# Clustered attention and a gated FFN on one core: from a hand-written step calendar to an operation graph that a list scheduler orders

## The chip, the cores and the metric

The kernel runs on one core of one Trainium2 chip. The metric is the device time of one launch in microseconds (us). The kernel before takes 378.75 us, the median of three runs (378.61 to 380.31). One execution was also recorded by the hardware profiler; all rows below are from that one, with a span of 378.3 us.

## What is computed

Four batches (B) of eight heads (H), 768 tokens (S), head size 64 (D). A query may attend to a key only when both pick the same one of 16 cluster centroids. The attention output, heads side by side, goes through a feed-forward network (FFN) with a sigmoid gate: 512 to 1536 and back to 512.

```
q_assign = argmax(q_n . c_n);  k_assign = argmax(k_n . c_n)      # normalised vectors
mask     = q_assign[:, :, :, None] == k_assign[:, :, None, :]
scores   = where(mask, q @ k.T / 8, -1e9)
attn     = softmax(scores) @ v
x        = attn, heads beside each other: (3072, 512)
out      = (sigmoid(x @ w_gate) * (x @ w_val)) @ w_out           # float32
```

## The kernel before

Tokens lie 128 to a partition block, so a head has six blocks of keys and six of queries. Two heads make a pair, four pairs a batch.

**Preparing a pair.** The raw keys and queries are split into a fp16 high part and a fp16 low part that lie beside each other in a tile `hl`: DVE makes the high part, POOL subtracts to get the low one (L212 and L215 in batch 0, L631 and L632 later). A DMA transpose from the SP queue turns `hl` to `T` (L222): 64 rows of high part, 64 of low part, tokens along the free axis. PE multiplies `T` with the centroids (`logits`, L229 and L238). DVE takes the maximum over 16 clusters and marks it as a one-hot `oh` (L256 to L265); the mark of a query is inverted and scaled by -1920. `oh` is turned too: by PE and a copy in batch 0 (L283, L530, L552), by a DMA transpose in the other batches (L645). Four small DMAs, `hop` (L287), then put 16 rows of it into rows 64 to 79 of `T`, over a part of the low rows that is no longer needed. A matmul over 80 rows then gives the scores with the mask in them.

**A step** is one block of 128 keys against three blocks of queries: one scores matmul of 384 columns (L419), one exponential of 128x384 on ACT (L424), and three matmuls with the values (L436) two steps later. There are 96 steps in a batch and 384 in all. At the end of a head DVE adds a tiny sum of all values (`sv`), takes the reciprocal (L197, L199), and POOL multiplies (L202). After a pair, SP issues a DMA transpose of the result into `xT` (L444).

**Batch 0** is cut in two. Steps 0 to 47 (A) use the first half of the queries, steps 48 to 95 (B) the second half. Each half has its own splits, DMA transposes (eight of nine blocks for A, four of six blocks for B), logits and hops. The very first pair puts its marks in place by PE and two copies instead of hops (`first_place`, L513 to L517).

**FFN.** It works on 384 tokens at a time, eight such halves in all. A gate unit (L301) is four matmuls of 384 columns, followed by a tanh on ACT (L307); a value unit (L316) likewise, followed by a multiplication on DVE (L321); there are 12 of each in a half. Then come nine output units of four matmuls of 512 columns (L333), and after every third one a copy (ACT L342 or DVE L340) and a store from SP (L343). Units are kept in a queue, and `ffn_run` issues some after every step, in proportion to the backlog.

**What sets the order.** Every engine runs its instructions in the order in which the program writes them. That order is written by hand: `run_steps` walks over the steps, and `at(i, f)` enters background work for step number i. Loads, DMA transposes, hops and stores all go through SP's one queue, weights and the first value loads through POOL's.

**PSUM** has eight banks: `ring` has four, `avp` two, `op` (FFN outputs) two.

Of the kernel before, what the change touches and what calls it, by code (L numbers as in the profile page):

```python
# [16 lines left out]
def kernel(  # L17
# [26 lines left out]

    def pool(name, bufs, **kw):
        return ctx.enter_context(
            tc.tile_pool(name=name, bufs=bufs, reuse_waits="tile", **kw)
        )
# [3 lines left out]
    rawp = pool("raw", 4)  # L52
    hlp = pool("hl", 4)
    tp = pool("T", 10)
    tbp = pool("TB", 4)
    vap = pool("va", 6)
    svp = pool("sv", 6)
    ohp = pool("oh", 2)
    esp = pool("es", 6)
    tmpp = pool("tmp", 2)  # L60
    xpp = pool("xp", 3)
    xtp = pool("xT", 2)
    htp = pool("hT", 2)
    thp = pool("th", 3)
    osp = pool("os", 3)
    smp = pool("sm", 3)
    ring = pool("ring", 4, space=bass.MemoryType.PSUM)
    avp = pool("avp", 2, space=bass.MemoryType.PSUM)
    op = pool("op", 2, space=bass.MemoryType.PSUM)

    def bank(n=512, dt=FP, name="bank"):
        return ring.tile([128, n], dt, tag="ring", name=name)


    ident = const.tile([128, 128], FP, name="ident")
    make_identity(nc, ident)
    identh = const.tile([128, 128], HP, name="identh")
    warm = const.tile([128, 512], HP, name="warm")
    POOL.memset(warm, 0.0)
    ones = const.tile([128, 128], HP, name="ones")  # L80
    POOL.memset(ones, 1.0)

    def raw(side):
        return rawp.tile([128, 2, NCH, 64], FP, tag=f"{side}raw", name=f"{side}raw")

    SRC = {"q": q, "k": k, "v": v}

    def view(side, b, p):
        return SRC[side][b, 2 * p : 2 * p + 2].rearrange("h (p c) d -> p h c d", c=NCH)

    RAW = {}

    def load(eng, side, b, p):
        t = RAW[side, b, p] = raw(side)
        eng.dma_start(out=t, in_=view(side, b, p))

    cen = const.tile([128, D], FP, name="cen")
    load(SP, "k", 0, 0)
    load(ACT, "q", 0, 0)
    SP.dma_start(out=cen, in_=centroids.rearrange("h c d -> (h c) d"))  # L100
    load(SP, "k", 0, 1)
    load(ACT, "q", 0, 1)


    WQ = 3
# [6 lines left out]
    def load_w(i):  # L112
        for t, src in ((wg[i], moe_w_gate), (wv[i], moe_w_val)):
            POOL.dma_start(
                out=t.rearrange("p dc fc f -> p dc (fc f)"),
                in_=src.rearrange("(dc p) (g f) -> p dc g f", p=128, f=WQ * 128)[:, :, i, :],
            )

    def load_wo(i):
        POOL.dma_start(  # L120
            out=wo[i],
            in_=moe_w_out.rearrange("(g fc p) m -> p g fc m", g=2, p=128)[:, i],
        )

# [5 lines left out]
    r1 = const.tile([128, 1], FP, name="r1")  # L130
    cm = const.tile([128, H, 2, NCL], HP, name="cm")

    def centroid_a():
        DVE.tensor_tensor(sq, cen, cen, ALU.mult)
        DVE.tensor_reduce(ss, sq, AX.X, ALU.add)
        ACT.activation(r0, ss, AF.Sqrt)
        ACT.activation(r1, warm[:, 0:1], AF.Exp)

    def centroid_b():
        DVE.tensor_scalar(r0, r0, 1e-6, None, ALU.add)  # L140
        DVE.reciprocal(r0, r0)
        for i in range(2):
            DVE.tensor_scalar(c2[:, i, :], cen, r0, None, ALU.mult)
        ct_ps = bank(128, name="ct_ps")
        PE.transpose(ct_ps, c2.rearrange("p a d -> p (a d)"), ident)
        cv = ct_ps.rearrange("p (h c) -> p h c", c=NCL)
        ACT.copy(cm[:, :, 0, :], cv)
        DVE.tensor_tensor(cm[:, :, 1, :], cv, cm[:, :, 0, :], ALU.subtract)


    VA, SV = {}, {}

    def v_cast(b, p):
        va = vap.tile([128, 2, NCH, 65], HP, name="va")
        VA[b, p] = va
        POOL.memset(va[:, :, :, 64:65], 1.0)
        POOL.tensor_copy(va[:, :, :, 0:64], RAW["v", b, p])

    def v_sum(b, p):
        s = svp.tile([128, 2, 65], HP, tag="vs", name="vs")  # L160
        POOL.memset(s[:, :, 64:65], float(NCH))
        with nc.allow_low_precision("sums of the fp16 values' sources"):
            DVE.tensor_reduce(  # L163
                s[:, :, 0:64], RAW["v", b, p].rearrange("p h c d -> p h d c"), AX.X, ALU.add
            )

        def rest():
            t = bank(130, name="vs_ps")
            PE.matmul(
                out=t, lhsT=ones, rhs=s.rearrange("p h d -> p (h d)"), start=True, stop=True  # L170
            )
            sv = svp.tile([128, 2, 65], FP, tag="sv", name="sv")
            SV[b, p] = sv
            DVE.tensor_scalar(sv.rearrange("p h d -> p (h d)"), t, TINY, None, ALU.mult)

        return rest

    def v_sum_pe(b, p):
        t = bank(130, name="vs_ps")
        for j in range(NCH):  # L180
            PE.matmul(
                out=t.rearrange("p (h d) -> p h d", h=2), lhsT=ones, rhs=VA[b, p][:, :, j, :],
                start=(j == 0), stop=(j == NCH - 1),
            )
        sv = svp.tile([128, 2, 65], FP, tag="sv", name="sv")
        SV[b, p] = sv
        DVE.tensor_scalar(sv.rearrange("p h d -> p (h d)"), t, TINY, None, ALU.mult)


    def bcast(ap, n):  # L190
        return ap.unsqueeze(len(ap.shape)).to_broadcast(list(ap.shape) + [n])

    def normalise(av, nq, b, p, e, x, eng=None):

        t = tmpp.tile([128, NCH, 65], FP, name="t")
        sv = SV[b, p][:, e, :].unsqueeze(1).to_broadcast([128, nq, 65])
        DVE.tensor_tensor(t[:, 0:nq, :], av, sv, ALU.add)  # L197
        rec = smp.tile([128, NCH], FP, name="rec")
        DVE.reciprocal(  # L199
            rec[:, 0:nq], t[:, 0:nq, 64:65].rearrange("p c x -> p (c x)")  # L200
        )
        (eng or POOL).tensor_tensor(x, t[:, 0:nq, 0:64], bcast(rec[:, 0:nq], 64), ALU.mult)  # L202
# [3 lines left out]
    T = {}  # L206

    def split(n, parts, lo_eng):

        hl = hlp.tile([128, n, 128], HP, tag="hl", name="hl")  # L210
        for o, r in parts:
            DVE.tensor_copy(hl[:, o : o + r.shape[1], 0:64], r)  # L212
        for o, r in parts:
            m = r.shape[1]
            lo_eng.tensor_tensor(  # L215
                hl[:, o : o + m, 64:128], r, hl[:, o : o + m, 0:64], ALU.subtract
            )
        return hl

    def turn(key, hl, pl):  # L220
        T[key] = pl.tile([128, hl.shape[1], 128], HP, tag="T", name="T")
        SP.dma_start_transpose(out=T[key], in_=hl.rearrange("p c x -> p (c x)"))  # L222

    def logits2(groups):

        lg = bank(512, name="lg2")
        for i, (t, c, h) in enumerate(groups):
            for s in range(2):
                PE.matmul(  # L229
                    out=lg[:, bass.ts(i, NCL)], lhsT=t[:, c, :], rhs=cm[:, h, s, :],  # L230
                    start=(i == 0 and s == 0), stop=(s == 1), skip_group_check=True,
                )
        return lg[:, 0 : len(groups) * NCL].rearrange("p (c n) -> p c n", n=NCL)

    def logits(t, h, n):
        lg = bank(512, name="lg")
        for c in range(n):
            PE.matmul(  # L238
                out=lg[:, bass.ts(c, 32)], lhsT=t[:, c, :],
                rhs=cm[:, h].rearrange("p s n -> p (s n)"), start=True, stop=True,  # L240
            )
        lv = lg[:, 0 : n * 32].rearrange("p (c s n) -> p c s n", s=2, n=NCL)
        lo = smp.tile([128, 12, NCL], FP, name="lglo")
        ACT.copy(lo[:, 0:n], lv[:, :, 1, :])  # L244
        return lv[:, :, 0, :], lo[:, 0:n]

    def pick(lg, parts):

        if isinstance(lg, tuple):
            ls = smp.tile([128, 12, NCL], FP, name="lgs")  # L250
            n = lg[0].shape[1]
            DVE.tensor_tensor(ls[:, 0:n], lg[0], lg[1], ALU.add)  # L252
            lg = ls[:, 0:n]
        n = lg.shape[1]
        mx = smp.tile([128, 18], FP, name="mx")
        DVE.tensor_reduce(mx[:, 0:n], lg, AX.X, ALU.max)  # L256
        for a, z, nh, key, o in parts:
            DVE.tensor_tensor(
                o,
                lg[:, a:z].rearrange("p (h c) n -> p h c n", h=nh),  # L260
                bcast(mx[:, a:z].rearrange("p (h c) -> p h c", h=nh), NCL),
                ALU.is_equal if key else ALU.is_lt,
            )
            if not key:
# [454 lines left out]
```

## Time and profile before

| | |
|---|---|
| median of the three runs | 378.75 us |
| span of the profiled execution | 378.3 us |
| busy: PE, ACT, DVE, POOL | 337.0, 230.4, 176.7, 113.6 us |
| mean granted clock of PE | 0.932 |
| first scores matmul (step 0) starts | 21.05 us |
| step 24, 48, 72 | 43.61, 63.21, 92.10 us |
| step 96 (second batch), 192, 288 | 111.61, 170.94, 247.69 us |
| last step ends, last matmul ends | 319.5, 374.5 us |

A step is said to start where its scores matmul starts in the trace. A busy PE is not PE at its peak: its clock can be at half rate ("granted clock" 0.50), and a matmul then takes twice as long. So a stage is read by three things together: how much of it PE was busy, at which clock, and what ended the idle time.

### The profile page before, as it was taken

Reading aid. Unit: us, or ns where it says so; the run is one execution under the profiler, and the core shown is the slowest. Engines: PE = TensorE matmul, PEld = TensorE weight load, DVE = VectorE, ACT = ScalarE, POOL = GpSimd, SP = SyncE. Lnnn points to the kernel's source line nnn. Section 1 sums busy time; section 2 is a strip of 40 time slices with the busy share of each in tenths; the row PEclk is TensorE's granted clock in tenths of the full one; section 3 lists DMA queues with packets and bytes.
Section 4 is the critical chain, followed back from the end, with each engine's and each line's share of the span. In section 5 each row is a group of like instructions: output and inputs, shape, how many; then the busy total and the mean of one; then the engine's idle time right before and its main releaser. Section 6 shows DMA issues by size and latency. Waiting matters only on the chain.

```text
span 378.3 us, 8520 instructions
## 1 busy us (share of the span) xinstructions
PE 337.0 (89%) x3177; PEld 205.5 (54%) x3177; DVE 176.7 (47%) x455; ACT 230.4 (61%) x527; POOL 113.6 (30%) x179
## 2 busy tenths in 40 slices
PE   3786955669999989889999999999999999999995
PEld 1354633436655556554666566656665566565552
DVE  3463532225563675662656365635563333242230
ACT  3044744437867878875787778758777787232231
POOL 3756566103342634523242423232401000000000
PEclk9975875559999999999999999999999999999999
DMA  5967999974766976966566539653523120300102
GB/s 186 253 187 150 226 179 197 239 137 144 110 175 143 215 187 126 224 165 174 146 148 177 114 88 231 178 139 81 87 52 73 51 36 2 105 1 30 55 2 83
DMA packets 96858, 50.07 MB, mean 132 GB/s; under 512 B 75376, under 2 KB 93424, under 8 KB 96816
## 3 DMA queue, kind: packets, MB, share of 16 engines
q1 hardware_dynamic: 90032, 42.44, 48.0%
q0 software_dynamic: 6240, 6.29, 9.6%
q10 hardware_dynamic: 544, 0.79, 0.6%
q8 instruction: 25, 0.41, 0.4%
q14 instruction: 17, 0.14, 0.1%
HBM read 28.34 MB, written 6.29 MB: 92 GB/s over the span
## 4 chain that ended last, share of the span: by engine, by line
PE 68%; DMA 14%; DVE 7%; issue 4%; POOL 3%; ACT 1%; SPq 1%; POOLq 0%; DVEq 0%
PE o L333 16%; PE v L316 15%; PE g L301 15%; DMA T<-hl 12%; PE sc L419 11%; PE av L436 6%; PE lg L238 2%; DMA T<-ohT 2%; PE wm L489 2%; DMA cen<-in_centroids_dram 1%; DVE hT L321 1%; POOL hl L215 1%; DVE vs L163 1%; DVE hl L212 1%; DVE t L197 1%
## 5 line engine op out<-in xcount | busy, mean ns | idle before, releaser
L424 ACT ACTIVATE es<-sc 128x384 f16<-128x384 f32 x384 | 174.2, 492 | 67.6 <-PE sc L419 54.5
L419 PE MATMUL sc<-T 80*128 80x384 f16 x384 | 124.3, 348 | 5.8 <-DMA T<-ohT 4.5
L436 PEld LDWEIGHTS <-es 128*128 128x128 f16 x1152 | 84.6, 102 | 51.0 <-ACT es L424 6.1
L436 PE MATMUL av<-va,es 128*128 128x65 f16 x1152 | 102.3, 200 | 1.4 <-ACT es L424 0.7
L321 DVE SCALAR_TENSOR_TENSOR hT<-th,v 128x384 f16<-128x384 f32 x96 | 53.0, 552 | 94.8 <-PE av L436 56.1
L202 POOL TENSOR_TENSOR xp<-t,rec 128x384 f16<-128x384 f32 (+1 forms) x40 | 28.3, 707 | 146.2 <-DVE rec L199 119.2
L333 PE MATMUL o<-wo,hT 128*128 128x512 f16 x288 | 70.3, 378 | 0.0
L307 ACT ACTIVATE th<-g 128x384 f32<-128x384 f32 x96 | 47.2, 492 | 28.5 <-DVE hT L321 16.2
L301 PE MATMUL g<-xTb,wg 128*128 128x384 f16 x288 | 58.6, 325 | 0.5 <-DVE hT L321 0.2
L316 PE MATMUL v<-xTb,wv 128*128 128x384 f16 x288 | 58.6, 325 | 0.3 <-DVE hT L321 0.3
L301 PEld LDWEIGHTS <-wg 128*128 128x128 f16 x384 | 37.7, 98 | 24.0 <-issue 3.8
L316 PEld LDWEIGHTS <-wv 128*128 128x128 f16 x384 | 37.5, 98 | 22.7 <-issue 2.5
L333 PEld LDWEIGHTS <-hT 128*128 128x128 f16 x288 | 27.8, 97 | 26.1
L419 PEld LDWEIGHTS <-T 80*128 80x128 f16 x384 | 38.3, 100 | 5.4 <-DMA T<-ohT 4.2
L632 POOL TENSOR_TENSOR hl<-kraw,hl 128x384 f16<-128x384 f32 x24 | 22.0, 917 | 31.4 <-issue 24.8
L197 DVE TENSOR_TENSOR t<-av,sv 128x390 f32<-128x390 f32 (+1 forms) x40 | 19.2, 479 | 22.9 <-PE av L436 22.9
L632 POOL TENSOR_TENSOR hl<-qraw,hl 128x384 f16<-128x384 f32 x24 | 21.9, 913 | 20.7 <-DVE hl L631 20.5
L342 ACT ACTIVATE ob<-o 128x512 f32<-128x512 f32 x16 | 9.6, 597 | 22.6 <-PE o L333 22.4
L163 DVE TENSOR_REDUCE vs<-vraw 128x128 f16<-128x768 f32 x12 | 17.6, 1466 | 0.0
L340 DVE TENSOR_SCALAR ob<-o 128x512 f32<-128x512 f32 x8 | 5.5, 692 | 25.6 <-PE o L333 25.6
L252 DVE TENSOR_TENSOR lgs<-lg,lglo 128x192 f32<-128x192 f32 x24 | 8.5, 355 | 17.8 <-ACT lglo L244 17.3
L229 PE MATMUL lg<-cm,T 128*128 128x16 f16 x192 | 6.5, 172 | 10.9 <-DMA T<-hl 10.9
(68 smaller groups left out, 241.8 us busy)
## 6 DMA issues: line engine op xcount, KB each, us to landing
kraw<-in_k_dram SPq DMA_DIRECT2D x16, 384.0 KB, 3.9
out_dram<-ob SPq DMA_DIRECT2D x24, 256.0 KB, 2.1
qraw<-in_q_dram SPq DMA_DIRECT2D x14, 384.0 KB, 4.1
vraw<-in_v_dram SPq DMA_DIRECT2D x12, 384.0 KB, 5.4
vraw<-in_v_dram POOLq DMA_DIRECT2D x4, 384.0 KB, 4.4
wg<-in_moe_w_gate_dram POOLq DMA_DIRECT2D x4, 384.0 KB, 8.2
wv<-in_moe_w_val_dram POOLq DMA_DIRECT2D x4, 384.0 KB, 9.6
wo<-in_moe_w_out_dram POOLq DMA_DIRECT2D x2, 768.0 KB, 13.6
```

The lines of the kernel that those rows point to most:

```text
L163: DVE.tensor_reduce(s[:, :, 0:64], RAW["v", b, p].rearrange("p h c d -> p h d c"), AX.X, ALU.add)
L197: DVE.tensor_tensor(t[:, 0:nq, :], av, sv, ALU.add)
L202: (eng or POOL).tensor_tensor(x, t[:, 0:nq, 0:64], bcast(rec[:, 0:nq], 64), ALU.mult)
L301: PE.matmul(out=g[:, 0:n], lhsT=wg[fc // WQ][:, dc, fc % WQ, :], rhs=xT[:, dc, t0 : t0 + n], start=(dc == 0), stop=(dc == NDC - 1),)
L307: ACT.activation(th[:, 0:n], g[:, 0:n], AF.Tanh, scale=0.5)
L316: PE.matmul(out=w[:, 0:n], lhsT=wv[fc // WQ][:, dc, fc % WQ, :], rhs=xT[:, dc, t0 : t0 + n], start=(dc == 0), stop=(dc == NDC - 1),)
L321: DVE.scalar_tensor_tensor(hT[:, fc, 0:n], st[0][:, 0:n], 1.0, w[:, 0:n], ALU.add, ALU.mult)
L333: PE.matmul(out=o, lhsT=hT[:, fc, bass.ts(t, 128)], rhs=wo[fc // 6][:, fc % 6, :], start=(fc == 0), stop=(fc == NFC - 1),)
L419: PE.matmul(out=sc.rearrange("p (c t) -> p c t", t=128), lhsT=s["k"], rhs=s["q"], start=True, stop=True,)
L424: ACT.activation(es, sc, AF.Exp, scale=SCALE)
L436: PE.matmul(out=av[:, s["c0"] + i, :], lhsT=s["es"][:, bass.ts(i, 128)], rhs=VA[b, p][:, e, s["j"], :], start=(first and i == 0), stop=(la ...
L632: POOL.tensor_tensor(hl[:, :, 64:128], r, hl[:, :, 0:64], ALU.subtract)
```

## The change

The whole order is made anew. Every piece of work becomes an `Op` with the engine or engines that may run it, a duration written by hand, the ops that it depends on, a priority, and tokens for the buffers that it takes. `schedule` then places the ops one after another while the program is built, and issues them in that order. Nothing of it runs on the chip. What else is different:

- Batch 0 is no longer cut in two. Its heads are turned with all 12 blocks by PE (`t_ps`, six transposes into a PSUM bank and a copy to `T` by DVE), not by DMA. The first pair's marks are placed by copies on DVE, those of the other three pairs by hops. Only the last pair of each batch is still worked in two halves of queries.
- `op` is gone: one ring of six banks serves scores, gates, values, outputs, logits and transposes; `av` keeps two.
- Loads of batches 1 to 3 are entered behind an attention step (`GATE`): 76 steps ahead for k and q, 56 for v. This is an order in the list, not a semaphore.
- The norm of the centroids is a power of one half on POOL (`ALU.pow`) in place of a square root on ACT; ACT loads one table of functions, not two. Before its first DMA issue ACT runs one exponential on a tile that DVE sets.
- The first q and k are loaded one head at a time; ACT's queue also brings the first v. All other loads of batch 0 come from SP; POOL loads only weights.
- The columns of ones in `va` and `vs` are set once; the one-hot tiles are cleared by DVE at the start. All copies of FFN outputs came out on ACT.
- Other buffers: `es` 8 (6 before), `hl` 5 (4), `xT` 3 (2), one-hot tiles 4 (3).
- Dummy matmuls (`wm`) of 256 columns are put in where the schedule shows PE idle for more than 0.25 us before its own time 13.0; 24 of them came out, against 26 of 512 columns before.

```diff
-    ring = pool("ring", 4, space=bass.MemoryType.PSUM)
-    avp = pool("avp", 2, space=bass.MemoryType.PSUM)
-    op = pool("op", 2, space=bass.MemoryType.PSUM)
+    NB = dict(
+        kraw=4, qraw=4, vraw=3, hl=5, T=10, vs=3, sv=5, ohT=3, es=8, t=3, x=3, xT=3, hT=2, th=3,
+        ob=3, sm=4, va=6, oh=4, scv=3, ring=6, av=2,
+    )
...
+    def schedule(free, slack, filler):
...
+        while cand:
+            opts = []
+            for o in cand:
+                tt = token_time(o) if o.acq else 0.0
...
+                for e, d in o.engs:
+                    r = tt
+                    for x in o.deps:
+                        soft = x in o.ord or (x.eng == e and x.xfer is None)
+                        r = max(r, x.end if soft else x.vis)
+                    opts.append((max(free[e], r), d, e, o))
+            t0 = min(x[0] for x in opts)
+            e0 = min((x for x in opts if x[0] == t0), key=lambda x: x[3].prio)[2]
+            near = [x for x in opts if x[2] == e0 and x[0] <= t0 + slack.get(e0, 0.0)]
+            s, d, e, o = min(near, key=lambda x: (x[3].prio, x[0], x[3].seq))
...
+        order.sort(key=lambda x: x[:2])
+        for _, _, fn, e in order:
+            fn(ENGS[e])
...
+    half = const.tile([128, 1], FP, name="half")
+    DVE.memset(half, 0.5)
+    spare = const.tile([128, 1], FP, name="spare")
+    ACT.activation(spare, half, AF.Exp)
...
-        ACT.activation(r0, ss, AF.Sqrt)
-        ACT.activation(r1, warm[:, 0:1], AF.Exp)
+        o = op_([("POOL", 0.5)], lambda g: g.tensor_tensor(r0, ss, half, ALU.pow), [o], -900)
...
+            if early:
+                outs = []
+                for side in range(2):
+                    mt = tok("ring")
+
+                    def turn(g, h=h, side=side):
+                        t = st["tps", h, side] = ps("ring", NCH * 128, HP, "t_ps")
+                        for c in range(NCH):
+                            g.transpose(t[:, bass.ts(c, 128)], HL[b, h][:, 6 * side + c, :], identh)
+
+                    def out(g, h=h, side=side):
+                        if side == 0:
+                            T[b, h] = sb("T", [128, 12, 128], HP)
+                        o = T[b, h][:, 6 * side : 6 * side + 6, :].rearrange("p c t -> p (c t)")
+                        cp(g, o, st["tps", h, side])
+
+                    o = op_(pe(0.36), turn, [los[h, side], IDENT], pr - 20, acq=[mt], use=[HLTOK[b, h]])
+                    eng = [("DVE", 0.47), ("ACT", 0.7)] if lead_in else dve(0.47)
...
+                o = op_(pe(0.165), sc, READY[b, h] + [SCPREV[0]], s, acq=[sct, scv], use=[TTOK[b, h]])
+                SCPREV[0] = STEP[s] = o
+                o = op_([("ACT", 0.375)], ex, [o], s, acq=[est], use=[sct, scv])
+                last = op_(
+                    pe(0.1), av, [o, VREADY[b, p], prev_av[0]], s + 1.5,
...
+            a = op_(pe(0.66), gate, XTREADY[b, hv] + [WG[fc // WQ], FFPREV[0]], base + 4 * fc, acq=[gt], use=[xt])
+            z = op_([("ACT", 0.375)], tanh, [a], -1, acq=[tht], use=[gt])
+            c = op_(pe(0.66), val, [a, WV[fc // WQ]], base + 4 * fc + 2, acq=[vt], use=[xt])
...
+    GK, GV = 76, 56
+
+    load("q", 0, 0, 0, ACTQ, -1000)
+    CEN = centroids_()
+    CM = CEN
+    load("k", 0, 0, 0, SPQ, -999)
+    load("q", 0, 0, 1, ACTQ, -998)
+    load("k", 0, 0, 1, SPQ, -998)
+    load("v", 0, 0, None, ACTQ, -997)
...
+    for b in range(B):
+        for p in range(NP):
+            U = 24 * (NP * b + p)
+            if b:
+                for side in "kqv":
+                    GATE[side, b, p] = STEP[max(0, U - GK if side != "v" else U - GV)]
+                    load(side, b, p, None, SPQ, U - 40 if side != "v" else U - 20)
+            pair_ops(b, p, b == 0, b == 0 and p == 0)
+            attend(b, p, p == NP - 1)
...
+    schedule(
+        {"PE": 1.2, "ACT": 1.8, "DVE": 2.4, "POOL": 1.8, "SP": 0.7},
+        {"PE": 0.0, "ACT": 0.02, "DVE": 0.02, "POOL": 0.02, "SP": 0.0},
+        filler,
+    )
```

## The prediction

> **What bounds the kernel now.** I read the table of stages first (length, then busy time of PE, weight loads, DVE, ACT, POOL, with instruction counts; granted clock; DMA share; GB/s).
>
> ```profile
> 25.00:30.00 5.00, 5.00 (x42) 3.65 (x40) 2.52 (x8) 3.44 (x8) 2.96 (x6) 0.50 0.53 178
> 30.00:40.00 10.00, 6.39 (x78) 4.76 (x78) 2.92 (x8) 3.48 (x8) 5.12 (x9) 0.50 0.96 161
> 40.00:50.00 10.00, 8.22 (x128) 5.58 (x126) 5.25 (x19) 7.36 (x17) 7.27 (x13) 0.94 1.19 217
> 50.00:60.00 10.00, 4.59 (x47) 3.17 (x46) 3.00 (x12) 3.65 (x8) 5.92 (x10) 0.57 1.30 198
> 60.00:70.00 10.00, 5.22 (x52) 3.30 (x51) 2.79 (x11) 3.90 (x9) 3.60 (x5) 0.50 1.25 197
> 70.00:80.00 10.00, 5.16 (x62) 3.70 (x61) 2.22 (x8) 3.99 (x9) 1.42 (x2) 0.50 1.12 238
> 200.00:220.00 20.00, 19.82 (x205) 12.28 (x202) 10.49 (x28) 14.76 (x36) 6.14 (x9) 1.00 0.56 138
> 320.00:340.00 20.00, 20.00 (x121) 11.05 (x120) 6.33 (x12) 5.96 (x12) 0.83 (x1) 1.00 0.16 51
> ```
>
> From 200 us on PE is full at full clock: nothing but less work helps there. From 25 to 80 us no engine is full, PE is mostly at half clock, and the DMA engines are busiest. The chain of waits names what ends last there (start, length, what), the timeline shows it on PE:
>
> ```profile
> 29.97 3.46 DMA T<-hl
> 39.10 4.37 DMA T<-ohT
> 58.23 21.27 DMA T<-hl x2
> 121.55 3.69 DMA T<-hl
> 163.33 4.68 DMA T<-hl
> ```
>
> ```profile
> 68.36 0.49 PE L229 MATMUL lg<-cm,T 128*128 128x16 f16 x12 [4.64 <-DMA T<-hl]
> 79.55 0.50 PE L238 MATMUL lg<-cm,T 128*128 128x32 f16 x12 [3.50 <-DMA T<-hl]
> ```
>
> So batch 0 waits for its own DMA transposes, and so, more weakly, does batch 1 up to 170 us. Step 0 starts at 21.05 and step 96 at 111.61.
>
> **Prices.** Scores to scores with the value matmuls between them take 0.26 us (229.62 to 229.88). A gate or value unit is 0.65, an output unit of four 0.865 (chain), 12 logits matmuls 0.35 (36 took 1.05). An exponential back to back is 4.78/11 = 0.435:
>
> ```profile
> 44.03 4.78 ACT L424 ACTIVATE es<-sc 128x384 f16<-128x384 f32 x11 [0.69 <-PE av L436]
> 44.12 0.50 PE L283 MATMUL oh_ps<-identh,oh 128*128 128x128 f16 x6
> L530 DVE COPY ohT<-oh_ps 128x768 f16<-128x768 f16 x3 | 1.7, 558 | 1.9 <-PE oh_ps L283 1.8
> ```
>
> The last two rows price the new work: six PE transposes 0.36 to 0.50 (their own pace and with drain), the copy out 0.56. I check the prices on the kernel before by counting, for each pair of heads (24 steps), what its order holds and taking the larger of PE and ACT. Pairs 8 to 15 come to 147.2 us; step 192 to 319.5 took 148.6, so a PE-bound stage runs at 1.01 of the sum. Pairs 4 to 7, where ACT is as loaded as PE, come to 51.2, and took 59.3 (111.61 to 170.94): 1.16, with the DMA waits in it.
>
> **Part 1, the start.** On ACT the square root, one table load (1.28) and its return go; a power on POOL comes, which no row shows: between a 128x1 activation's 0.20 and POOL's 0.91 for 128x384. I take 0.3, nearer to the small shape, and it lies beside the first split. Against that, ACT's first load is issued only after DVE has cleared `warm` and four one-hot tiles and set `half`. POOL's clearing of one such tile took 0.74, a 128x64 multiplication on DVE 0.23, so four cost 0.9 to 3.0; I take 1.6 in about 3.3 us instead of 0.73 for q's issue, landing near 8 after the 5.0 that q took (less for half the size). Then DVE's queue up to the first marks: high q, a low k, centroids, T copy, low q twice with a high part, T copy, high, copy, high, maximum, two marks, high, maximum, two marks, two placing copies = 0.35+0.55+0.29+0.56+0.55+0.35+0.55+0.56+0.35+0.56+0.35+0.35+0.50+0.35+0.35+0.50+1.12 = 8.2, plus some 1.3 for the round trips to PE: step 0 at 17.5 us, 3.5 earlier. Bounds: 15.5 (short clears, load lands at 6) and 19.5 (long clears, port waits such as 1.03 us for a 0.35 us high part at 12.94).
>
> **Part 2, batch 0.** Twelve DMA transposes go from SP (eight of nine blocks, four of six; 1.2 to 1.5 us of issue and a median 3.8 to landing each), and eight of its 20 hops. What comes for 96 steps: ACT 96 x 0.435 = 41.8. PE: 96 x 0.26 = 25.0, 12 + 1 further turns and three of marks 16 x 0.4 = 6.4, six heads of 24 logits 4.2, six and more small ones 2.5: 38. DVE, counted in its order: 12 T copies 6.7, 21 high parts at 0.45 9.5, eight heads' maxima and marks 7.3, one-hots 1.7, ends of heads 8.1, two value sums 2.9, rest 3.5: 40. POOL: 21 low parts at 0.915, six multiplications, four casts, nine weight DMA issues at 0.8: 35. Three engines sit within 10% of each other in a fixed order, so the stage can't run at 41.8. Times the 1.16 of pairs 4 to 7 it is 48.5; more engines are tight here, and I take 54. Low end 46. High end: PE at half clock all the way, 96 x 0.486 (28.39 to 28.87 us) plus twice the turns 12.8 plus logits and small ones 9: 68, of which I hold 64, as at 41.2 the clock returned after 4 us of full PE. The DMA room is not free: nine loads, ten weight DMAs (4.7 MB) and batch 1's transposes use it, but nothing in batch 0 but hops waits for it. At the end SP holds the hops of pair 4 behind the last `xT` transpose, whose x ends 1.2 us after step 95: 1.2 + 1.3 + 1.1 + 2 = 5.6 us, covered by the seven gate and seven value units that stand there: 14 x 0.65 = 9.1. Without that cover it would be 5.6 of plain wait.
>
> The trace speaks on the clock before any rule: it fell at 24.1 us, in a stretch where PE's longest idle was 0.82 us. [...]
>
> **Part 3, steps 96 to 383.** Per pair, the larger of PE and ACT: 12.4, 12.4, 20.9, 19.8; 16.3, 21.7, 15.7, 23.9; 12.3, 22.5, 15.1, 14.0 = 207.0 (the third: 24 x 0.26 + 14 x 0.65 + 5 x 0.865 + 3 x 0.35 = 20.8). The ring is no larger: 6 banks against 4 + 2. The three pairs that ACT bounds (37.1) get the 1.16: 6 more. FFN units stand in blocks at the end of pairs, which costs ACT time that the mean hides: 2. All 24 output copies on ACT add eight of 0.60, where it has room. So 215; bounds 207 and 226 (half of the pairs at 1.16 or a little more).
>
> **Part 4, the end.** After step 383 both orders hold 48 gate and value units and 27 output units, 54.9 us (319.5 to 374.5), then 3.8 for copy, store and end.
>
> Sum: 17.5 + 54 + 9.1 + 215 + 54.9 + 3.8 = 354.3, against the 378.3 of the same execution; the median stands 0.45 above that. I say 354. Check by difference: step 0 comes 3.5 earlier; batch 0 held 18.2 us of FFN in 90.6, so 72.4 of attention becomes 54, 18.4 less; the rest holds 9.1 more FFN and is 6.6 longer, 2.5 less. Together 24.4.
>
> **Rivals.**
> - *The order holds as drawn* (no coupling loss): 15.5 + 46 + 9.1 + 207 + 54.9 + 3.8 = 336. For it: from 200 us on the old order loses 1%. Against: written durations are short (0.375 for an exponential that takes 0.435, 0.28 for high parts at 0.35 to 0.56), so the real engines drift out of the drawn order.
> - *Batch 0 is only rebound*: PE leaves the DMA wait and meets DVE at half clock. 19.5 + 64 + 9.1 + 219 + 54.9 + 3.8 = 370. For it: DVE's 40 in 41.8, banks that PE can refill only after a late DVE copy. Against: PE at 38 dense recovers its clock.
> - *SP's queue turns slower than before*: one in-order queue holds hops behind `xT` transposes and stores that wait for POOL and ACT. Twelve pairs from step 96 begin with hops; each must be late by 2.0 us beyond its cover to eat the 24. Beyond that it is slower; at 3 us it is 354 + 36 = 390. For it: transposes took up to 12.3 us to land, and SP was held 9.21 in one issue. Against: the old order had the same queue and the same twelve sets of hops, and PE waited for `T<-ohT` only 4.5 us in all, three times.
> - *Gating does nothing*: it is an order, not a wait, and SP's queue decides anyway. Same time as the forecast; the loads would stand earlier in the trace than 76 steps.
>
> **How the numbers follow.** Forecast 354 (345 to 364) 0.5; order as drawn 0.17; rebound 0.2; slower 0.1; 0.03 is left near no change. 336 to 376 leaves out a little of the first and the slow case. One half per cent is what a measurement here tells from no change: faster 0.87, same 0.02, slower 0.11.
>
> **What would show it.** No `T` DMA transpose before step 40; step 0 at 17 to 18; step 95 at 70 to 74 with granted clock 1.00 after some 5 us; step 96 near 81 with gate units before it; ACT idle in batch 0 put down to DVE copies rather than DMA; 54.9 us after the last step. Wrong, if PE's waits from step 96 name hops or DMA by over 10 us, or if the clock stays at 0.50 past 40 us.

## The result, and the profile after

The changed kernel takes 364.87 us, the median of four runs (361.28 to 367.25), against 379.53 us for the kernel before on the same chip: 0.958 of the time, with an interval of 0.952 to 0.964. It is faster, as forecast, but by 14.7 us and not by 24.4: 0.958 of the 378.75 us on which the forecast stood is 362.9 us, near the upper end of its range of 345 to 364. The slowest of the four runs counts as one in a slower state and is left out of the interval; the median of the other three is 363.26 us, so that a difference from the kernel after is sure to some 2 us only. The profiled execution of it took 363.26 us, with a span of 361.5; its sum by the terms of the prediction is:

| term | predicted | measured | difference |
|---|---|---|---|
| step 0 starts | 17.5 | 16.14 | -1.4 |
| steps 0 to 95 (16.14 to 75.6) | 54 | 59.5 | +5.5 |
| FFN units ahead of step 96 (75.6 to 93.75) | 9.1 | 18.1 | +9.0 |
| steps 96 to 383 (93.75 to 302.7) | 215 | 209.0 | -6.0 |
| FFN after the last step | 54.9 | 54.9 | 0 |
| copy, store and end | 3.8 | 3.8 | 0 |

So the two terms that came out too long, 14.5 us together, lie between 16 and 94 us. The table of stages of the kernel after, in the columns of the one above (start and end, length, busy PE, weight loads, DVE, ACT, POOL with counts, granted clock, DMA share, GB/s):

```profile
30.00:40.00 10.00, 7.65 (x127) 6.32 (x126) 5.09 (x13) 5.47 (x13) 6.06 (x9) 0.83 1.10 188
40.00:50.00 10.00, 9.45 (x154) 6.40 (x152) 6.80 (x18) 8.78 (x22) 6.62 (x9) 1.00 1.09 176
50.00:60.00 10.00, 5.70 (x61) 2.47 (x57) 4.45 (x11) 6.58 (x18) 6.71 (x8) 0.99 1.32 210
60.00:70.00 10.00, 5.66 (x61) 3.96 (x62) 4.20 (x10) 5.35 (x12) 2.47 (x3) 0.67 1.30 198
70.00:80.00 10.00, 6.49 (x76) 4.16 (x73) 7.01 (x21) 6.16 (x14) 3.61 (x4) 0.83 1.29 190
80.00:90.00 10.00, 8.05 (x45) 4.16 (x45) 5.65 (x13) 2.28 (x5) 2.89 (x4) 0.66 1.09 225
90.00:100.00 10.00, 10.00 (x100) 6.54 (x98) 4.32 (x11) 7.27 (x18) 1.56 (x2) 1.00 0.67 120
```

The half clock of the old batch 0 is mostly gone up to 60 us. From 50 to 90 us, though, no engine is full, and from 50 to 80 us the DMA share is the highest of the run. What PE waits for there stands in brackets in the timeline of PE (start, length, work, idle time before it and what ended it):

```profile
33.90 0.32 PE L644 MATMUL sc<-T 80*128 80x384 f16 x1 [2.35 <-DMA T<-ohT]
62.33 0.50 PE L471 MATMUL lg<-cm,T 128*128 128x32 f16 x12 [6.42 <-DMA T<-hl]
69.74 0.23 PE L601 MATMUL vs_ps<-vs,ones 128*128 128x130 f16 x1 [1.96 <-DVE vs L595]
79.90 0.47 PE L471 MATMUL lg<-cm,T 128*128 128x32 f16 x12 [3.26 <-DMA T<-hl]
83.27 0.48 PE L776 MATMUL g<-xT,wg 128*128 128x384 f16 x1 [1.95 <-DMA xT<-x]
84.83 1.49 PE L776 MATMUL g<-xT,wg 128*128 128x384 f16 x4
93.75 0.65 PE L644 MATMUL sc<-T 80*128 80x384 f16 x3
```

The five waits are 15.9 us, about the 14.5 that the two terms lost. (The match is rough: the prediction left room for some waiting, and the half clock adds to the loss.) Two of the waits stand before logits of batch 1's first two pairs. In PE's in-order queue the logits at 62.33 sit ahead of scores of batch 0 (62.81), those at 79.90 ahead of the FFN units (80.22). The last two lines show a gate unit at half clock (1.28 us to the start of the next unit, against 0.65 at full clock) and step 96, which follows the units without a gap. The DVE wait behind the third is one more transfer, a value load, which the chain of waits shows with its 11.69 us (start, length, what):

```profile
41.02 6.51 DMA vraw<-in_v_dram
56.51 11.69 DMA vraw<-in_v_dram
79.64 3.59 DMA xT<-x
```

The queue of SP in the same stretch (start, time that the issue held SP, what):

```profile
59.53 13.56 SPq L444 DMA_TRANSPOSE T<-hl  x2
82.06 6.55 SPq L444 DMA_TRANSPOSE T<-hl  x2
90.04 2.96 SPq L558 DMA_DIRECT2D T<-ohT  x4
```

Two transposes held SP for 13.56 us. The marks of the pair that begins at step 96 were done on DVE at 66.2, but their turn stood behind these two and an `xT` and was issued at 75.90; two more transposes then held SP for 6.55, and the hops left at 90.04. The two that step 96 needs had landed by 92.50; what it then waited for was the end of the FFN units in PE's queue.

### The profile page after: what moved, and what is told of

Same layout as the page of the kernel before. It is cut to its first block, busy times and chain, and to the rows that moved or that the text cites. A ratio compares the mean times of both kernels' runs of the same rounds, so it can differ in the third digit from the quotient of the medians.

```text
span 361.5 us, 8703 instructions
## 1 busy us (share of the span) xinstructions
PE 329.2 (91%) x3259; PEld 206.6 (57%) x3259; DVE 188.6 (52%) x470; ACT 224.3 (62%) x533; POOL 99.2 (27%) x129
## 3 DMA queue, kind: packets, MB, share of 16 engines
q1 hardware_dynamic: 78208, 40.84, 48.5%
## 4 chain that ended last, share of the span: by engine, by line
PE 74%; DMA 13%; DVE 9%; issue 2%; SPq 1%; ACT 1%; POOL 0%; ACTq 0%; POOLq 0%
PE g L776 16%; PE v L788 16%; PE o L817 15%; PE sc L644 15%; PE av L657 8%; DMA T<-ohT 5%; DMA vraw<-in_v_dram 5%; DVE hl L238 2%; PE lg L471 2%; DMA qraw<-in_q_dram 1%; DVE vs L595 1%; DMA xT<-x 1%; DVE T L238 1%; PE t_ps L423 1%; DVE oh L371 1%
## 5 line engine op out<-in xcount | busy, mean ns | idle before, releaser
L651 ACT ACTIVATE es<-sc 128x384 f16<-128x384 f32 x384 | 164.3, 503 | 37.2 <-PE sc L644 26.2
L644 PE MATMUL sc<-T 80*128 80x384 f16 x384 | 108.6, 336 | 5.2 <-DMA T<-ohT 4.5
L657 PEld LDWEIGHTS <-es 128*128 128x128 f16 x1152 | 73.5, 99 | 38.2 <-ACT es L651 8.7
L657 PE MATMUL av<-va,es 128*128 128x65 f16 x1152 | 92.6, 197 | 0.7 <-ACT es L651 0.2
L776 PE MATMUL g<-xT,wg 128*128 128x384 f16 x384 | 79.6, 330 | 2.0 <-DMA xT<-x 2.0
L788 PE MATMUL v<-xT,wv 128*128 128x384 f16 x384 | 79.3, 330 | 0.8 <-DVE hT L796 0.8
L783 ACT ACTIVATE th<-g 128x384 f32<-128x384 f32 x96 | 47.9, 499 | 48.5 <-PE g L776 28.3
L690 POOL TENSOR_TENSOR x<-t,rec 128x384 f16<-128x384 f32 x24 | 20.6, 858 | 100.1 <-DVE rec L683 65.9
L238 POOL CAST va<-vraw 128x768 f16<-128x768 f32 x16 | 13.3, 833 | 47.6 <-DMA vraw<-in_v_dram 32.8
L595 DVE TENSOR_REDUCE vs<-vraw 128x128 f16<-128x768 f32 x12 | 17.9, 1493 | 13.0 <-DMA vraw<-in_v_dram 12.9
L238 DVE CAST hl<-qraw 128x384 f16<-128x384 f32 x32 | 18.9, 605 | 3.2 <-DMA qraw<-in_q_dram 3.2
L471 PE MATMUL lg<-cm,T 128*128 128x32 f16 x288 | 11.0, 177 | 9.7 <-DMA T<-hl 9.7
```

The lines of the kernel that those rows point to most:

```text
L238: (eng.copy if eng is ACT else eng.tensor_copy)(o, i)
L595: g.tensor_reduce(s[:, :, 0:64], RAW["v", b, p].rearrange("p h c d -> p h d c"), AX.X, ALU.add)
L644: g.matmul(out=t.rearrange("p (c t) -> p c t", t=128), lhsT=T[b, h][0:80, j, :], rhs=T[b, h][0:80, 6 + 3 * i : 9 + 3 * i, :], start=True, ...
L651: g.activation(st["es", key], st["sc", key], AF.Exp, scale=SCALE)
L657: g.matmul(out=st["av", u][:, c0 + c, :], lhsT=st["es", key][:, bass.ts(c, 128)], rhs=VA[b, p][:, e, j, :], start=(n == 0 and c == 0), sto ...
L690: g.tensor_tensor(st["x"][:, q0 : q0 + nq, bass.ts(e, 64)], st["t", u][:, 0:nq, 0:64], bcast(st["rec", u][:, 0:nq], 64), ALU.mult,)
```

## The experiments

All were run against the kernel before on the same chip (379.1 to 379.6 us there). The "kernel after" is at 364.9.

**PE turns only the first pair.** Pairs 1 to 3 of batch 0 go back to the DMA transpose; the scheduler, ring, gates and all else stay.

```diff
-            if early:
+            if early and p == 0:
```

> The changed kernel with pairs 1 to 3 of batch 0 turned by DMA transposes again, everything else as it is (the scheduler places them). Theory of the turning: the changed kernel gains because six DMA transposes of 12 blocks and what waits for them left batch 0; then step 96 falls from 93.75 back to 102 or later, PE waits for T<-hl before step 96 more than the 9.7 us of the changed kernel, and the time is 372 to 382 against its 365. Rival, the order: the scheduler's order brings the gain and hides transposes as well as PE turns; then 360 to 369.

Measured: 375.04 us (373.82 to 376.87), 0.990 (0.986 to 0.994), inside the range of the theory; PE's logits wait for `T` again (23.8 us in the whole run, 9.7 in after), as the timeline shows twice in batch 0:

```profile
37.94 0.81 PE L457 MATMUL lg<-cm,T 128*128 128x16 f16 x24 [4.05 <-DMA T<-hl]
51.56 0.81 PE L457 MATMUL lg<-cm,T 128*128 128x16 f16 x24 [6.98 <-DMA T<-hl]
```

The theory's mark for step 96 (102 or later) was missed: it started at 92.04. In this order no FFN units stand ahead of it, where after has 14, while steps 0 to 95 took 75.3 us instead of 59.5. In the scheduled order turning by PE is worth 10.2 us.

**PE turns, in the order written by hand.** The kernel before, with its twelve transposes of batch 0 replaced by PE turns and DVE copies at the same places; the copy of the identity matrix that the turns need moves ahead of the first.

```diff
-        turn(("A", h), ahl[h], tp)
+        turn_pe(("A", h), ahl[h], tp)
...
-        turn(("B", p), st0["bhl", p], tbp)
+        turn_pe(("B", p), st0["bhl", p], tbp)
```

> The kernel before, in its hand-written order and with its halves of queries, with only the twelve transposes of batch 0 made by PE and copied by DVE. Theory of the turning: the waits for T<-hl up to 80 us (some 22 us of idle PE in 25 to 80) go for the most part and the clock falls less; step 96 at 92 to 100 instead of 111.6 and a time of 360 to 370. Rival, the order: the waits move to the copies on DVE, the hops and the low parts, and the time stays at 373 to 380.

Measured: 384.14 us (383.58 to 388.52), 1.017 (1.012 to 1.023): slower by 1.7%, so the expectation fell, and the rival's too. The chain of waits shows one reason that is of the experiment's own making (start, length, what):

```profile
17.91 1.14 PE t_ps L227 x9
19.05 3.99 PE wm L501 x14
23.04 0.45 PE lg L241 x18
```

The 14 dummy matmuls that used to fill the wait for the DMA transpose now stand between the turn and its logits. Step 0 starts at 26.48, 5.4 later than before; from there to the start of step 96 it takes 3.7 us less than before (86.9 against 90.6), and from step 96 to step 192 2.1 more. Less the dummies' 4.0 us it would be 380.1, by subtraction alone: no gain to see. Of these two orders, the turns pay only in the one that was drawn around them. I did not try a hand order re-planned for them.

**No gates.** The loads of batches 1 to 3 are free to go as soon as a buffer is.

```diff
-                    GATE[side, b, p] = STEP[max(0, U - GK if side != "v" else U - GV)]
```

> The changed kernel without the gates: loads of batches 1 to 3 are entered as soon as a buffer is free. My prediction said that the gates do nothing: 361 to 369, loads earlier in the SP queue. Rival: the earlier loads take the DMA engines from hops and first transposes and the time rises to 370 or more; or they bring v in time and it falls to 355 to 360.

Measured: 380.77 us (377.80 to 384.81, ten runs), 1.002 (0.999 to 1.005), in the first rival's range. The whole gain is gone. Steps 0 to 95 take 67.5 us (59.5 with gates), and step 96 starts at 113.37. SP's queue shows what the early loads do:

```profile
58.83 6.64 SPq L444 DMA_TRANSPOSE T<-hl  x1
70.97 13.32 SPq L444 DMA_TRANSPOSE T<-hl  x1
108.39 2.44 SPq L558 DMA_DIRECT2D T<-ohT  x4
```

One transpose held SP for 13.32 us, and the hops for step 96 left at 108.39.

**The ring cut back to four banks**, with two for the FFN outputs as before the change.

```diff
-        ob=3, sm=4, va=6, oh=4, scv=3, ring=6, av=2,
+        ob=3, sm=4, va=6, oh=4, scv=3, ring=4, op=2, av=2,
...
-            ot, obt = tok("ring"), tok("ob")
+            ot, obt = tok("op"), tok("ob")
```

> The changed kernel with the ring cut back to four banks and two banks for FFN outputs alone. Theory: six banks were used before too, so the split costs little: 363 to 370. Rival: one ring of six lets batch 0, where no outputs are written, use two banks more; with four, turns, logits and scores wait for each other, step 48 moves from 46.2 to 52 or later and the time is 372 to 385.

Measured: 372.91 us (370.97 to 375.66), 0.986 (0.981 to 0.991): 8.0 us slower than after, at the edge where the rival's range begins. Step 48 came at 54.80 (46.25 in after), which the rival had asked for. In its profile, which is of the slowest of its four runs (375.66), the clock stayed at half for some 27 us of the start, which makes the share of the ring uncertain (more on that in the last section).

**The weights moved.** The eight gate and value weight loads follow steps 2 to 23, those of the output steps 98 and 110. (The ten are 4.7 MB, as the prediction has it, not the 3.7 of the text below.)

```diff
-                    weights(i, w, -500 + n, [STEP[2 + 8 * n]])
+                    weights(i, w, -500 + n, [STEP[2 + 3 * n]])
             for i in range(2):
-                weights_out(i, -490 + i, [STEP[66 + 12 * i]])
+                weights_out(i, -490 + i, [STEP[98 + 12 * i]])
```

> The kernel after, with the FFN's weight loads moved out of the crowded stage: the eight gate and value loads follow steps 2, 5, ..., 23 in place of 2, 10, ..., 58, the two output weights steps 98 and 110 in place of 66 and 78 (3.7 MB in all, 2 MB of it gone from 35 to 72 us). Theory (batch 0 and the block behind it are late because the DMA engines are full: share 1.09 to 1.32 from 30 to 90 us, so that T<-hl of batch 1 and the v loads land late): the 9.7 us in which lg waits for T<-hl falls under 5, the 12.9 us in which the value sums wait for vraw under 6, step 96 comes at 84 to 89 us instead of 93.75, time 355 to 361. Rival (the loads of batches 0 and 1 are themselves what fills the engines, and what is late is late by SP's order): waits within 2 us of those of after, step 96 at 92 to 96, time 363 to 367.

Measured: 359.06 us (357.46 to 360.38), 0.949 (0.945 to 0.952), the best of all and inside the theory's range. The stage in which it gains most, and SP's queue there:

```profile
50.00:60.00 10.00, 9.49 (x123) 5.00 (x121) 5.67 (x19) 9.87 (x27) 4.65 (x6) 1.00 0.94 192
```

```profile
48.21 1.54 SPq L444 DMA_TRANSPOSE T<-hl  x1
50.89 1.53 SPq L444 DMA_TRANSPOSE T<-hl  x1
59.36 5.40 SPq L444 DMA_TRANSPOSE T<-hl  x2
69.48 3.53 SPq L444 DMA_TRANSPOSE T<-hl  x1
```

From 50 to 60 us the DMA share is 0.94 (1.32 in after) and PE busy 9.49 (5.70). The first six `T<-hl` of batch 1 held SP for 14.4 us in all; in after it was 25.5 (1.89 + 3.47 + 13.56 + 6.55), without gates 31.4. Logits, which waited 6.42 and 3.26 us in after, wait for `T` 0.24 and 0.95 there. Steps 0 to 95 take 54.4 us. Of the theory's two waits only one went: DVE still waits 10.4 us for value loads. And step 96, due at 84 to 89 and here at 78.64, is 15 us earlier mostly because 11 of the 14 FFN units that stood ahead of it (7.2 us of work) now stand behind it.

**Value loads earlier**, released 76 steps ahead like keys and queries.

```diff
-    GK, GV = 76, 56
+    GK, GV = 76, 76
...
-                    load(side, b, p, None, SPQ, U - 40 if side != "v" else U - 20)
+                    load(side, b, p, None, SPQ, U - 40)
```

> The kernel after, with the value loads of batches 1 to 3 released with the queries and keys (76 steps ahead of use instead of 56) and given their priority; the buffers (3) stay. Theory (the value sums stand at the head of DVE's in-order queue and wait 12.9 us for loads issued late; PE then waits 2.2 us for them and the FFN's products stand behind): that wait falls under 5 us, step 96 comes 2 to 5 us earlier, time 359 to 363. Rival (the value loads then take the place of keys and queries on a full set of DMA engines and the wait moves to kraw or qraw, or to T<-hl): sum of the DMA waits of DVE and PE unchanged or larger, time 364 to 370.

Measured: 365.04 us (363.62 to 367.45), 0.964 (0.958 to 0.970), no change. DVE's wait for `vraw` fell from 12.9 to 3.4 us, but the waits of its high parts for kraw and qraw came to 13.8 (4.6 in after), as the rival had it: the two together are 17.2 us against 17.5, and step 96 came at 98.06, later than in after. Here the order of the loads chose who waits, not how much.

**Planned durations and planned landings.** Thirteen of the written durations are set to measured ones; in another kernel the latencies of transfers are.

```diff
-                o = op_([("ACT", 0.375)], ex, [o], s, acq=[est], use=[sct, scv])
+                o = op_([("ACT", 0.43)], ex, [o], s, acq=[est], use=[sct, scv])
...
-                    use=[HLTOK[b, h]], xfer=0.8, lat=2.4,
+                    use=[HLTOK[b, h]], xfer=0.8, lat=5.0,
```

> The kernel after, with thirteen of the durations that the scheduler plans by set to those of the profile of after (exponential 0.375 to 0.43 us, high parts on DVE 0.28 to 0.45, one-hot comparisons 0.18 to 0.29, products' combination 0.47 to 0.55, and so on); only the order changes, no operation. Theory (the order is drawn for a machine some 10 % too fast on DVE and ACT, so that PE's static queue puts the scores ahead of what is ready and the FFN behind): steps 96 to 383 take 209 now and 200 to 206 with it, time 355 to 361. Rival (order is limited by landings of transfers, which these durations leave as they are; a list scheduler's order hardly moves with them): within 2 us of after, 362 to 367.

> The kernel after, with the latencies that the scheduler plans by for transfers set near those of the profile of after (T<-hl 2.4 to 5.0 us behind its transfer, loads of batches 1 to 3 1.9 to 4.5, ohT and xT 2.4 to 3.5); only the order changes. Theory (PE waits 9.7 us for T<-hl and DVE 12.9 us for vraw because their in-order queues were drawn with landings too early, and other ready work stands behind them): both waits fall under half, step 96 comes 3 to 6 us earlier, time 356 to 362. Rival (what follows needs those transfers anyway; the wait moves to the scores): 363 to 368.

Measured: durations 363.55 us (361.88 to 364.38), 0.959 (0.955 to 0.962), no change; steps 96 to 383, which the theory wanted shorter than 209, took 218.4, with step 96 at 84.38 and no FFN units ahead of it. Landings: 365.8, 372.0, 372.1 and 372.4 us, too scattered for a verdict, and in no run below the median of after. Truer numbers for the planner didn't make a better order.

**Both: weights moved and durations as measured** (the two edits above).

> The kernel after, with the FFN's weights moved (as in e5_weights_moved, 359.1 us) and the thirteen measured durations (as in e7_durations_measured, 363.6 us, not told apart from after). Theory (what the crowding cost was not the order's doing, and the order planned by truer durations gives a little on top once transfers land on time): 353 to 358. Rival (the durations only shuffle the order and the outcome is e5's within its spread): 357 to 361.

Measured: 361.37 us (358.42 to 363.23), 0.952 (0.946 to 0.958). That can't be told from the moved weights alone, as the rival said. It also bears on the moved weights: with the measured durations in both, the same move gave 2.2 us (363.55 to 361.37), inside the spread, and not 5.8. Steps 0 to 95 took 9.2 us less (58.0 against 67.2), but steps 96 to 383 took 226.5 against 218.4.

**Weights moved, and pair 4 turned by PE too.**

```diff
-            pair_ops(b, p, b == 0, b == 0 and p == 0)
+            pair_ops(b, p, b == 0 or (b, p) == (1, 0), b == 0 and p == 0)
```

> The kernel after, with the FFN's weights moved and the first pair of batch 1 treated like the pairs of batch 0: turned by PE and copied by DVE, its one-hots too; only the hops into T and the xT turns of it stay with SP. It takes two T<-hl and one ohT<-oh transposes out of SP's queue between 48 and 66 us, and adds some 24 + 6 PE turns (2.6 us at the 0.50 us that six took), 24 more logit matmuls of half width and five DVE copies (2.8 us at 0.56). Theory (SP's in-order queue, in which T<-hl took 1.5 to 5.4 us each to issue ahead of the hops, is what made the block ahead of step 96 long): step 96, at 78.6 in e5_weights_moved, comes at 73 to 77, time 354 to 358. Rival (PE is the bound from here on, 91 % busy, so what it does more it pays in full): step 96 moves by under 2 us, time 359 to 364.

Measured: 368.27 us (364.89 to 369.84), 0.972 (0.967 to 0.977), 9.2 slower than with the weights moved alone. Neither expectation holds whole, and the time lies above both ranges: step 96 started at 70.21, earlier than the theory asked, and still the last step started at 303.6 instead of 296.4. Three FFN units went behind step 96, PE was busy 1.8 us longer (331.9 against 330.1), and DVE waited 17.5 us for value loads against 10.4.

**Weights moved, gates at 60 and 48 steps, and at 92 and 72.**

```diff
-    GK, GV = 76, 56
+    GK, GV = 60, 48
```

> The kernel after, with the FFN's weights moved and the loads of batches 1 to 3 gated 60 steps ahead of use for keys and queries, 48 for values, in place of 76 and 56. Theory (loads that stand in SP's queue early hold the hops up, as without any gate, 380.8 us; 60 steps of some 0.55 us are 33 us, and a load, its split, its turn, the logits, the one-hots and their hops took about 25): 355 to 359. Rival (what bounds a load is the buffers, and later loads only put the wait before the high parts, with kraw and qraw waits of over 8 us in place of 4): 360 to 368.

> The kernel after, with the FFN's weights moved and the loads of batches 1 to 3 gated 92 steps ahead of use for keys and queries, 72 for values (76 and 56 gave 359.1 us, 60 and 48 gave 376.2, no gate with the weights where after has them 380.8). Theory (two costs stand against each other: gated late, loads land after their high parts are due, e11's 11.9 us wait for kraw; gated early, they fill SP's queue and the DMA engines ahead of the hops, as without a gate; 76 is near the balance): 360 to 370, with fewer waits for kraw and qraw and more for T<-hl or T<-ohT. Rival (only lateness costs; the raw buffers hold the loads back before they can crowd anything): 354 to 359.

Measured: 376.20 us (373.75 to 379.97), 0.989 (0.985 to 0.993) for the late gates and 373.89 us (371.83 to 376.62), 0.988 (0.984 to 0.993) for the early ones. With 76 and 56 it is 359.06. Both times lie above every range that was expected. Waits of the late gates, in a profile of their 379.50 us run (engine, line, what it waited for: us in total, times, longest):

```profile
DVE hl L238 <- DMA kraw<-in_k_dram: 16.8, 5, 11.9
PE g L776 <- DVE lgs L486: 10.6, 1, 10.6
```

Waits of the early ones:

```profile
DVE vs L595 <- DMA vraw<-in_v_dram: 22.6, 9, 4.8
PE sc L644 <- DMA T<-ohT: 8.9, 7, 3.2
```

Late gates do what the rival said, at a higher price: the high parts wait for keys, once for 11.9 us, and the FFN's gate units wait 10.6 us for the addition of the late logits. Early gates lose too, but not where I expected: the first six `T<-hl` held SP for 10.7 us, less than in after, without gates or with the weights moved alone, and it is the value loads that come late. The chain has one of 8.80 us at 76.98. So 76 is near the best of the three, and the price on each side is 15 to 17 us; that crowding is the whole price on the early side isn't shown.

## Why the prediction was right, and where it was not

*The direction and most of the size* came from batch 0's DMA transposes, and in the scheduled order that holds: put back, they cost 10.2 of the 14.7 us. In the order by hand the turns alone gained nothing, and without the gates the whole gain went, so they are needed and not enough.

*The start* was sized well: the four clears took 1.60 us (1.6 taken), q landed at 8.1 ("near 8"), and the power on POOL took 0.78 where I took 0.3, ahead of 2.44 us in which DVE waited for q anyway. Of what the prediction calls port waits the trace shows the times only: in the kernel before a high part of 128x384 took 0.34 to 0.36 us where POOL was idle, and where POOL worked beside it mostly that too, but up to 1.03; why is not shown. The 1.4 us by which step 0 came earlier lie behind q: 8.0 us from its landing to step 0, where I counted 9.5.

*Batch 0, +5.5.* The step that failed is "nothing in batch 0 but hops waits for it", it being the room on the DMA engines. Logits of batch 1 and value sums wait for DMA too, and in PE's queue they stand ahead of batch 0's scores (6.42 and 1.96 us in the lines above). The prediction's own rows had it: the logits at 79.55 (L238, 128x32) are batch 1's, so the second transpose in the chain's 21.27 us, and PE's 3.50 us, were no transpose of batch 0's. I had counted the ten weight loads and the transposes that use that room and priced them at nothing. With eight weights moved ahead and two behind, the stage took 54.4, near the 54 of the prediction. That is no proof of the 54, which was taken above the 48.5 that the factor of 1.16 gives, and DVE still waited for value loads there. That DVE's queue and half clock set the end, the "rebound" rival, is not what the waits name: DMA is, behind 11.0 of PE's 14.6 us of idle time from step 0 to step 95 (2.35 of it for hops, 2.2 behind a value sum on DVE).

*The block, +9.0.* I covered the hops' 5.6 us with 9.1 us of units. The hops, and the turn of the marks ahead of them, came not behind one `xT` transpose but behind four transposes of the next pairs as well, and the units themselves waited 3.26 us for logits in front of them and 1.95 for `xT`, and ran at half clock up to 87 us. So the 18.1 us are the 9.1 of units, 5.2 of these waits, 2.5 of half clock and 1.4 of value matmuls and logits. The cover was late for the same reason as the thing that it was to cover.

*Steps 96 to 383, -6.0.* 209.0 against counted work of 207.0: the 1.16 that I put on the pairs that ACT bounds, and the 2 for units in blocks, were not due. Hops after step 96 were covered (PE waited 4.5 us for hops in the whole run, 2.1 of it from step 96 on); the rival with a slower SP queue fell there, though its mechanism was at work before step 96.

*"Gating does nothing"* fell plainest: without gates the time is 380.8. That it is "an order, not a wait" is true, and in an in-order queue the order is the wait. *"The ring is no larger"*, costed at nothing, was 8.0 us with the reserve noted.

Of the marks named for the prediction, the end (54.9) was met and step 0 came earlier still; step 95 (75.3 for 70 to 74) and step 96 (93.75 for 81) missed. ACT's idle time in batch 0 is put down to PE and not to DVE copies. Neither sign of being wrong showed, as both looked away from where the time went: PE's waits were due from step 96 on, and they came before it. One reading of the rows was also off, without weight in the sum: from 25 to 30 us PE was full (5.00 of 5.00 at half clock).

*The argument against the order as drawn*, that its durations are short, fell as well: true durations left the time as it was.

The parts do not add: turns 10.2, gates 15.9 and ring 8.0 make 34, more than the whole change. Each experiment draws a new order. Where nothing but the order changed, the time stayed (durations) or scattered from 365.8 to 372.4 (landings). So these are the prices of taking a part out of this order, not of the part itself. That the sum of the stages, 354.3, came within 7.2 us of the 361.5 is luck in part: 14.5 us too little in two terms met 7.4 too much in two others.

Two prices of a DMA transpose came out apart. By landing it is like a load in the kernel after: in the first 100 us the median from issue to landing was 6.8 us for `T<-hl` and 6.7 to 7.7 for loads of 384 KB from SP. In the kernel before it was 3.9, shorter transposes among them, against 4.2 to 6.3. By what it costs the queue that issues it, it is not: in the same 100 us of after a load held SP for 0.4 to 1.5 us and a transpose of twelve blocks for 1.5 to 9.7 (1.5 to 3.5 with the weights moved, 1.3 to 13.3 without gates). The DMA share alone doesn't set that. In the kernel before, the four transposes of six blocks held SP for 1.24 to 1.32 us between 43 and 65 us, at shares of 1.19 to 1.30 in the table, and the next one, of twelve blocks, for 9.21:

```profile
62.79 1.30 SPq L222 DMA_TRANSPOSE T<-hl  x1
67.16 9.21 SPq L222 DMA_TRANSPOSE T<-hl  x1
```

Whether shorter transposes would have let the hops through in the new order was not tried.

## What to carry to other kernels

When transposes, hops and loads share one in-order queue, price a transfer by how long it holds that queue while the DMA engines are full (here 1.3 to 13.3 us for a transpose of twelve blocks), and write down who stands behind it; DMA engines with room in the mean (a share of 0.60 over the run of the kernel after) had none in that stretch (1.29 to 1.32 from 50 to 80 us). Move large transfers that nobody is waiting for (here weights) out of the stage in which small ones are due: two constants were worth 5.8 us in this order (2.2, inside the spread, in the one with measured durations). And don't take an early step for progress when other work has been moved past it: count the work done on the engine that binds.

## What the runs showed of the hardware

A busy PE alone did not bring the clock back. In the kernel with four banks, whose PE first stood idle for 4.22 us, the table of stages reads, in the columns above:

```profile
20.00:22.00 2.00, 2.00 (x15) 1.43 (x14) 1.47 (x3) 1.27 (x3) 1.69 (x2) 0.50 1.05 162
22.00:24.00 2.00, 2.00 (x36) 1.49 (x34) 1.83 (x4) 1.43 (x4) 1.98 (x4) 0.50 0.51 76
24.00:26.00 2.00, 2.00 (x25) 1.16 (x22) 2.00 (x2) 1.14 (x4) 1.71 (x2) 0.50 0.63 36
36.00:38.00 2.00, 2.00 (x38) 1.83 (x36) 1.32 (x4) 0.49 (x1) 0.00 (x0) 0.90 0.37 75
```

It held 0.50 from 10 to 36 us, although PE was full for 6 us on end from 20, and for another 8 from 28 (in the trace's busy time, whose ends are modelled; a scores matmul took 0.51 us there and 0.33 at full clock, and from one scores matmul to the next, with the value matmuls between them, it is 0.49 against 0.26). In the kernel after the clock went to 1.00 at 12 us, after 3 us of the same work, and fell to 0.50 at 36 us behind an idle stretch of 2.35. No one length of idle or of busy time fits all of this: the clock fell behind 2.35 us of idle time there and behind no more than 0.82 in the kernel before, and it came back after 3 us of work there and not for 26 us here. What sets its fall and its return is left open.
